# Eight float32 heads instead of ten, and a second set of probability tiles for the others

## The chip, the cores and the metric

The kernel runs on one core of a Trainium2 chip. The metric is the device time of one execution in microseconds (us); the time before is the median of three runs.

## The reference

A block-causal attention (4 batches, 8 heads, 576 positions, 64 wide, blocks of 64) is followed by two dense layers without gates between them: the first squares a ReLU, the second applies a rational function of the hidden value. All data is float32.

```python
def _attn_ref(q, k, v):                      # each (4, 8, 576, 64)
    scores = scale * np.matmul(q, k.transpose(0, 1, 3, 2))
    mask = block_i >= block_j                # blocks of 64
    scores = np.where(mask, scores, -1000000000.0)
    scores = scores - np.max(scores, axis=-1, keepdims=True)
    attn = np.exp(scores)
    attn = attn / (np.sum(attn, axis=-1, keepdims=True) + 1e-09)
    return np.matmul(attn, v)

def _moe_ref(x, w_in, w_out):                # 2304 tokens, 512 -> 2048 -> 512
    h = np.maximum(x @ w_in, 0.0)
    return h * h @ w_out

def _moe2_ref(x, w_in, w_out, a, b):
    h = x @ w_in
    P = a[0] + a[1] * h + a[2] * h * h + a[3] * h ** 3
    Q = 1.0 + np.abs(b[0]) * np.abs(h) + np.abs(b[1]) * h * h
    return (P / (Q + 1e-06)) @ w_out
```

## The kernel before, in words

TensorE multiplies in two ways here. A float32 product keeps its operands as they are. A split product works on a high part in the type fp32r and a remainder (x = high + low), and adds two or three cheaper products. The heads 0 to 9 (PLAIN, L30) are float32 heads ("plain"), the heads 10 to 31 and both dense layers are split.

Attention runs in slots. A slot is one group of query tiles of one head: `GROUPS` (L42) has four, the tiles (0, 1), 2, 3 and 4. The eight heads of batch 0 are visited twice, first for groups 0 and 1 (slots 0 to 15), then for groups 2 and 3 (slots 16 to 31). From then on a head takes four slots: head h has the slots 4h to 4h + 3, up to slot 127. Score tiles are named after their slot: sy68 or sx69 belongs to slots 68 and 69, which are head 17.

The loop at L578 writes down, for slot i: the scores (`emit_s`, TensorE), the division by the row sums of slot i - 1 (`emit_norm`, GpSimd for split heads), the row maximum (`emit_max`, VectorE), the exponential (`emit_exp`, ScalarE, into the probability tiles p0 to p4), the product with the values for slot i - 4 (`emit_pv`), and the transposes of the probabilities of slot i - 3 (`emit_t`, TensorE, copied by ScalarE and, for split heads, a low part taken by VectorE into `pt`). The loads of the following heads and the preparation of their operands (`prep_qk`, `prep_v`) stand in the same loop. A split head costs ScalarE two copies (L234, L235), VectorE one remainder (L238), GpSimd one remainder (L240) and two operations on the values (L249, L251).

The first half of the first dense layer (`moe_a`, hidden units 0 to 1023) is poured in between: `advance` (L544) emits so many steps of three products at each slot, batch by batch. Batch 0 starts at slot 20 (`FIRST`), batches 1, 2 and 3 at the slots 68, 100 and 132. The attention output of a batch, `xt`, is filled head pair by head pair; the hidden products (ha, L482) of a batch read all four pairs in turn, so the last quarter of each waits for the last two heads of the batch. There are two banks of PSUM for these products ("mm", L253).

`convA` (a `Converter`, L81) unpacks the 16 weight tiles of that half, four VectorE operations each (L118 to L122), two ScalarE operations and one on GpSimd. `due` (L562) says at which slots it takes a step: 0.3 steps a slot up to slot 20, then 0.5.

Two sets of probability tiles exist (`psets`, L141), and `ptile` (L158) picks one: heads 0 to 7 take turns, all heads from 8 on use set 0. After slot 36 the pool with the second set, "early", is released (`make_two`, L200), and the tiles q_two and k_two of the split heads take its place.

The program is written in this order, and a scheduler places each engine's instructions from it; each engine then runs its own in the order that results. All loads are issued on SyncE's queue (SP), the first k alone on ScalarE's.

Of the kernel before, what the change touches and what calls it, by code (L numbers as in the profile page):

```python
# [17 lines left out]
P = 128  # L18
# [10 lines left out]
SCALE = 0.125  # L29
PLAIN = 10  # L30
SUBS = ((0, 320), (320, S))
# [5 lines left out]
LN63 = 63.0 * 0.6931471805599453  # L37
MASKED = -1.0e30

# [5 lines left out]
def f(ap):  # L45
    return ap.bitcast(F32)
# [3 lines left out]
def attention_moe_moe(ctx: ExitStack, tc: tile.TileContext, q, k, v, wi1, wo1, wi2, wo2, a, b, out):  # L50
# [107 lines left out]
    def ptile(un, t):  # L158
        own = psets[un.hd % 2 if un.hd < H else 0]
        if un.gis == (0, 1) and un.hd % 4 > 1:  # L160
            return own[4][:, 0:3 * P] if t == 2 else own[3][:, P * t:P * (2 * t + 1)]
        return own[t]
# [9 lines left out]
    class Visit:  # L172
        def __init__(self, n, hd, at, gis):
# [5 lines left out]
            self.k1 = SUB if gis == (0, 1) else S  # L179

    def load_qk(un, eng=nc.sync):
        if len(un.gis) == 2 and un.n % 4 > 1:
# [8 lines left out]
        for q0, q1, k0, k1 in cuts:  # L191
            nc.sync.dma_start(un.qr[:, q0:q1], q[un.hd][:, q0:q1])
            eng.dma_start(un.kr[:, k0:k1], k[un.hd][:, k0:k1])

# [4 lines left out]

    def make_two(un):  # L200
        early.release()
        late = tc.alloc_tile_pool(name="late", bufs=1, reuse_waits="tile")
        for n in range(2):
            q_two.append(late.tile([P, SP], F32R, name=f"q_two{n}"))
            k_two.append(late.tile([P, S], F32R, name=f"k_two{n}"))
            nc.scalar.activation(q_two[n][D:P], un.qr[D:P], AF.Copy)
            nc.scalar.activation(k_two[n][D:P], un.kr[D:P], AF.Copy)
        return late

    def load_v(un):  # L210
        src = v[un.hd].rearrange("p (c d) -> p c d", d=D)
        if un.plain:
            if un.hd % 2 == 0:
                un.vs = attn.tile([P, 5, P], F32, tag="vs", name=f"vs{un.n}", bufs=2)
            else:
                un.vs = units[un.n - 1].vs
            o = D * (un.hd % 2)
            nv = 3 if un.gis == (0, 1) else 5
            nc.sync.dma_start(un.vs[:, 0:nv, o:o + D], src[:, 0:nv])
        else:  # L220
            un.vr = attn.tile([P, 5, D], F32, tag="vr", name=f"vr{un.hd}", bufs=1)
            nc.sync.dma_start(un.vr, src)

    def prep_qk(un, step):
        if un.plain:
            if step == 0 and un.scale == 1.0:
                cols = un.qr[:, un.q0:un.q1]
                nc.gpsimd.tensor_scalar(cols, cols, SCALE, 0.0, op0=ALU.mult, op1=ALU.add)
            return
# [36 lines left out]
    def emit_s(i):  # L266
# [12 lines left out]
        for t in g:  # L279

            cols = slice(P * t, P * (t + 1))
            if un.plain:
                products = [(un.qr[:, cols], un.kr)]
            else:
                products = [(un.qh[:, cols], un.kk), (un.q2[:, cols], un.k2)]
# [126 lines left out]
    def emit_pv(un, half):  # L412
# [13 lines left out]
        if un.plain:  # L426
            for i, (c, src, dst, width) in enumerate(PV[half]):
                for n_, o in enumerate((0, D)):
                    nc.tensor.matmul(ps[o:o + D, dst:dst + width], un.vs[:, c, o:o + D],
                                     un.pt[:, n_, ROW[c], src:src + width],  # L430
                                     start=i == 0, stop=i == len(PV[half]) - 1)
# [127 lines left out]
    AHEAD = 0  # L559
    R1, R2, RS = 0.3, 0.5, 20  # L560

    def due(i):  # L562
        return int(i * R1) if i < RS else int(RS * R1 + (i - RS) * R2)

# [13 lines left out]
    for i in range(NI + 5):  # L578
# [21 lines left out]
        advance(steps(i + 1) - steps(i + 0.5), gate)  # L600
        if i == 4 * PLAIN - 4:
            late = make_two(slots[i][0])
        for back in range(4):
# [16 lines left out]
    if MOE_AT > 4:  # L620
        moes.append(moe_a(B - 1))
    late.release()
    attn.release()
# [261 lines left out]
```

## Time and profile before

| what | us |
|---|---|
| three runs: median (lowest to highest) | 1025.94 (1022.83 to 1026.55) |
| the profiled execution, whole | 1022.03 |
| the profiled execution, span from first to last instruction | 1020.2 |
| slots 0 to 19 and start, no dense layer (0 to 41.2) | 41.2 |
| slots 20 to 39 (41.2 to 93.8) | 52.6 |
| slots 40 to 47, the first two split heads (93.8 to 121.8) | 28.0 |
| slots 48 to 127 (121.8 to 349.3) | 227.5 |
| the rest of attention, `moe_a` of batch 3 (349.3 to 417.8) | 68.5 |
| second half of the first layer, second layer (417.8 to 1020.2) | 602.4 |

A row of the page's first part is an engine's busy time, its share of the span and its instructions. The stretches of the table are cut where a slot's first score product starts on TensorE. TensorE's busy time is modelled at the ends of its products, so a busy TensorE can still be waiting a little; an idle gap before an instruction is shown with what released it.

### The profile page before, as it was taken

The numbers are of one execution on the slowest core, as the hardware profiler recorded it, in microseconds if no ns is written. First come the engines' busy times: TensorE is split into PE (matmuls) and PEld (weight loads), VectorE is DVE, ScalarE is ACT, GpSimd is POOL, SyncE is SP. The second block draws the span as 40 slices with busy tenths as digits, with TensorE's granted clock in tenths as the row PEclk, the third lists the DMA queues.
The fourth block names the chain that finished last, engine by engine and source line by source line (L and its number), as shares of the span: only waits on it lengthen the run. The fifth ranks groups of instructions, "written<-read, shape, count | busy, mean of one in ns | idle before, by whom it ended". The sixth has DMA issues, their size and how long they took to land. (4 is left out here: it accounts for less than half of the span.)

```text
span 1020.2 us, 17058 instructions
## 1 busy us (share of the span) xinstructions
PE 995.7 (98%) x5721; PEld 884.1 (87%) x5721; DVE 727.6 (71%) x1412; ACT 722.2 (71%) x1620; POOL 582.6 (57%) x632
## 2 busy tenths in 40 slices
PE   7999999999999999999999999999999999999997
PEld 5677999999999999999788888887888888899996
DVE  6798587768767646786667666887766766777766
ACT  7779687768777746564455557787787776788775
POOL 5677686768676745630232448767466554655552
PEclk9999999999999999999999999999999999999999
DMA  9766334243432204457655572001101100100000
GB/s 302 221 201 210 120 99 150 92 117 111 118 93 81 67 31 149 167 193 247 234 174 187 171 249 95 1 1 41 42 1 32 42 1 1 50 24 1 32 1 31
DMA packets 63894, 106.58 MB, mean 104 GB/s; under 512 B 16064, under 2 KB 34496, under 8 KB 63808
## 3 DMA queue, kind: packets, MB, share of 16 engines
q1 hardware_dynamic: 63520, 105.34, 32.0%
q8 instruction: 45, 0.74, 0.3%
q14 instruction: 41, 0.34, 0.1%
q10 hardware_dynamic: 288, 0.16, 0.1%
HBM read 79.17 MB, written 23.07 MB: 100 GB/s over the span
## 5 line engine op out<-in xcount | busy, mean ns | idle before, releaser
L816 PE MATMUL yc<-w_co,gc 128*128 128x512 f32 x864 | 211.8, 391 | 3.1 <-ACT gc L776 3.1
L707 PE MATMUL hc<-xc,w_ci 128*128 128x512 f32 (+1 forms) x960 | 211.2, 368 | 0.0
L707 PEld LDWEIGHTS hc<-xc,w_ci 128*128 128x128 f32 x960 | 176.1, 188 | 26.3
L816 PEld LDWEIGHTS yc<-w_co,gc 128*128 128x128 f32 x864 | 161.1, 188 | 36.0 <-ACT gc L776 4.6
L777 POOL TENSOR_TENSOR gc<-t,gc 128x512 fp32r<-128x512 f32 (+1 forms) x78 | 105.0, 1353 | 126.1 <-issue 103.3
L482 PE MATMUL ha<-xt,w_ai 128*128 128x320 f32 (+1 forms) x768 | 123.1, 305 | 0.8 <-POOL xt L451 0.6
L495 PE MATMUL ya<-ga,w_ao 128*128 128x320 f32 (+1 forms) x768 | 117.6, 302 | 3.5 <-ACT r L508 1.9
L482 PEld LDWEIGHTS ha<-xt,w_ai 128*128 128x128 f32 x768 | 107.8, 189 | 5.8 <-issue 3.0
L802 POOL TENSOR_TENSOR wq<-wq,ab 128x512 f32<-128x512 f32 (+1 forms) x78 | 96.4, 1235 | 28.7 <-ACT wq L800 28.7
L495 PEld LDWEIGHTS ya<-ga,w_ao 128*128 128x128 f32 x768 | 107.7, 192 | 5.2 <-ACT r L508 2.1
L747 PE MATMUL yb<-gb,w_bo 128*128 128x512 f32 (+1 forms) x480 | 105.9, 368 | 1.1 <-DVE yp L752 1.1
L707 PE MATMUL hb<-xb,w_bi 128*128 128x512 f32 (+1 forms) x480 | 105.5, 367 | 0.0
L747 PEld LDWEIGHTS yb<-gb,w_bo 128*128 128x128 f32 x480 | 87.6, 188 | 13.1 <-ACT gb L509 1.5
L776 ACT ACTIVATE gc<-t 128x512 fp32r<-128x512 f32 (+1 forms) x80 | 47.1, 589 | 72.9 <-DVE t L785 72.9
L803 DVE TENSOR_TENSOR t<-hc,t 128x512 f32<-128x512 f32 (+1 forms) x80 | 50.9, 636 | 66.0 <-ACT t L801 66.0
L707 PEld LDWEIGHTS hb<-xb,w_bi 128*128 128x128 f32 x480 | 87.4, 188 | 11.2
L356 POOL TENSOR_SCALAR p<-p,stat 64x64 f32<-64x64 f32 (+4 forms) x110 | 62.2, 567 | 43.4 <-DVE stat L352 15.8
L370 PE MATMUL tp<-ident,p 128*128 128x128 f32 x480 | 79.2, 281 | 1.1 <-DVE pt_plain L390 0.7
L783 DVE SCALAR_TENSOR_TENSOR wq<-wq,ab 128x512 f32<-128x512 f32 (+1 forms) x80 | 55.2, 691 | 33.8 <-ACT ab L782 21.9
L402 DVE TENSOR_TENSOR pt<-tp,pt 128x384 fp32r<-128x384 f32 (+3 forms) x176 | 58.8, 366 | 20.3 <-ACT pt L400 17.5
L400 ACT ACTIVATE pt<-tp 128x384 fp32r<-128x384 f32 (+3 forms) x176 | 53.8, 346 | 24.4 <-PE tp L370 22.9
L785 DVE SCALAR_TENSOR_TENSOR t<-t,coef,ab 128x512 f32<-128x512 f32 (+1 forms) x80 | 66.8, 835 | 1.7
(137 smaller groups left out, 1983.2 us busy)
## 6 DMA issues: line engine op xcount, KB each, us to landing
kr<-in_k_dram SPq DMA_DIRECT2D x32, 288.0 KB, 3.8
raw_ci<-in_wi_dram SPq DMA_DIRECT2D x16, 512.0 KB, 4.4
raw_co<-in_wo_dram SPq DMA_DIRECT2D x16, 512.0 KB, 3.6
qr<-in_q_dram SPq DMA_DIRECT2D x24, 320.0 KB, 3.3
raw_ai<-in_wi_dram SPq DMA_DIRECT2D x8, 512.0 KB, 4.8
raw_ao<-in_wo_dram SPq DMA_DIRECT2D x8, 512.0 KB, 4.4
raw_bi<-in_wi_dram SPq DMA_DIRECT2D x8, 512.0 KB, 3.5
raw_bo<-in_wo_dram SPq DMA_DIRECT2D x8, 512.0 KB, 3.4
```

The costliest lines, as they stand in the source:

```text
L356: nc.gpsimd.tensor_scalar(pv, pv, st[r:P, 6 + n:7 + n], 0.0, op0=ALU.mult, op1=ALU.add)
L370: nc.tensor.transpose(ps[:, P * n:P * (n + 1)], ptile(slots[i][0], t)[:, P * c:P * (c + 1)], ident)
L402: nc.vector.tensor_tensor(low, src, f(high), op=ALU.subtract)
L482: nc.tensor.matmul(ps[:, 0:n], w[:, zw, P * kk:P * (kk + 1)], xt[:, zx, kk, first:end], start=i == 0, stop=i == 3 * KK - 1)
L495: nc.tensor.matmul(ps[:, 0:n], wA["o", m][:, zw, P * c:P * (c + 1)], gs[m][:, zg, 0:n], start=i == 0, stop=i == 3 * HALF - 1)
L707: nc.tensor.matmul(ps[:, 0:n], w[:, zw, P * kk:P * (kk + 1)], xt[:, zx, kk, 0:n], start=i == 0, stop=i == 3 * KK - 1)
L747: nc.tensor.matmul(acc[j, c][:, 0:n], wB["o", m][:, zw, P * c:P * (c + 1)], g[:, zg, 0:n], start=m == 0 and i == 0, stop=last and i == 2)
L777: (nc.vector if u - 2 >= len(units) - END else nc.gpsimd).tensor_tensor(g[:, 1, 0:n], t, f(g[:, 0, 0:n]), op=ALU.subtract)
L783: nc.vector.scalar_tensor_tensor(w, w, Q0, r, op0=ALU.add, op1=ALU.mult)
L785: nc.vector.scalar_tensor_tensor(t, t, a0, r, op0=ALU.add, op1=ALU.mult)
L802: (nc.vector if u >= len(units) - END else nc.gpsimd).tensor_tensor(w, w, ab, op=ALU.mult)
L816: last = nc.tensor.matmul(acc[j, c], g[:, zg, P * c:P * (c + 1)], w3["o", m][:, zw, :], start=m == 0 and i == 0, stop=m == NM - 1 and i == 2)
```

## The change

The number of float32 heads goes from ten to eight (heads 8 and 9 become split heads). For the float32 heads the loads and products of q and k use 80 partitions (64 of data and 16 of marks for the mask) instead of 128. The values of a float32 head are loaded as one run of 768 or 1280 bytes a partition instead of runs of 256. `due` becomes one rate, 0.45. The second set of probability tiles stays to the end of attention and all heads take turns. q_two and k_two get places of their own from the start; their mark halves are loaded from DRAM at slot 16 (four loads, four ScalarE copies, two copies by DMA) instead of being copied by ScalarE at slot 36. The mask value becomes a power of two.

```diff
-PLAIN = 10
+PLAIN = 8
-MASKED = -1.0e30
+MASKED = -(2.0 ** 100)
     def ptile(un, t):
-        own = psets[un.hd % 2 if un.hd < H else 0]
+        own = psets[un.hd % 2]
+            self.rows = D + 16 if hd < PLAIN else P
-            nc.sync.dma_start(un.qr[:, q0:q1], q[un.hd][:, q0:q1])
-            eng.dma_start(un.kr[:, k0:k1], k[un.hd][:, k0:k1])
+            nc.sync.dma_start(un.qr[0:un.rows, q0:q1], q[un.hd][0:un.rows, q0:q1])
+            eng.dma_start(un.kr[0:un.rows, k0:k1], k[un.hd][0:un.rows, k0:k1])
-    def make_two(un):
-        early.release()
-        late = tc.alloc_tile_pool(name="late", bufs=1, reuse_waits="tile")
+    def make_two():
         for n in range(2):
-            q_two.append(late.tile([P, SP], F32R, name=f"q_two{n}"))
-            k_two.append(late.tile([P, S], F32R, name=f"k_two{n}"))
-            nc.scalar.activation(q_two[n][D:P], un.qr[D:P], AF.Copy)
-            nc.scalar.activation(k_two[n][D:P], un.kr[D:P], AF.Copy)
-        return late
+            q_two.append(attn.tile([P, SP], F32R, name=f"q_two{n}"))
+            k_two.append(attn.tile([P, S], F32R, name=f"k_two{n}"))
+        for two, src, w_ in ((q_two, q, SP), (k_two, k, S)):
+            for lo in range(0, w_, SUB):
+                hi = min(lo + SUB, w_)
+                raw = attn.tile([P, SUB], F32, tag="tmp", name=f"marks{w_}_{lo}", bufs=2)
+                nc.sync.dma_start(raw[D:P, 0:hi - lo], src[0][D:P, lo:hi])
+                nc.scalar.activation(two[0][D:P, lo:hi], raw[D:P, 0:hi - lo], AF.Copy)
+            nc.sync.dma_start(f(two[1][D:P]), f(two[0][D:P]))
-                un.vs = attn.tile([P, 5, P], F32, tag="vs", name=f"vs{un.n}", bufs=2)
+                un.vs = attn.tile([P, 2, 5 * D], F32, tag="vs", name=f"vs{un.n}", bufs=2)
-            o = D * (un.hd % 2)
-            nv = 3 if un.gis == (0, 1) else 5
-            nc.sync.dma_start(un.vs[:, 0:nv, o:o + D], src[:, 0:nv])
+            nv = D * (3 if un.gis == (0, 1) else 5)
+            nc.sync.dma_start(un.vs[:, un.hd % 2, 0:nv], v[un.hd][:, 0:nv])
-                products = [(un.qr[:, cols], un.kr)]
+                products = [(un.qr[0:un.rows, cols], un.kr[0:un.rows])]
-    R1, R2, RS = 0.3, 0.5, 20
+    RATE = 0.45
     def due(i):
-        return int(i * R1) if i < RS else int(RS * R1 + (i - RS) * R2)
+        return int(i * RATE)
-        if i == 4 * PLAIN - 4:
-            late = make_two(slots[i][0])
+        if i == 4 * H // 2:
+            make_two()
-    late.release()
+    early.release()
     attn.release()
```

The order of the instructions moves with it. TensorE's order where the dense layer passes from batch 0 to batch 1: ha1 are hidden products of batch 1, sx and sy scores (of slots 70 to 73 here), tp the transposes of a slot, pv15 the value product of head 15, the last of batch 0. Before:

```order
L482 MATMUL ha1_0_1_2563<-xt1_1342,w_ai1_349 128x320 x11
L442 MATMUL pv15_1_2476<-pt_1438,vs15_2289 128x192
L370 MATMUL tp64_0_2493<-ident_70,p0_1_91 128x128
L370 MATMUL tp64_0_2493<-ident_70,p1_1_94 128x128
L442 MATMUL pv15_1_2476<-pt_1438,vs15_2289 128x64
L370 MATMUL tp64_0_2493<-ident_70,p1_1_94 128x128
L370 MATMUL tp65_0_2532<-ident_70,p2_1_96 128x128 x3
L482 MATMUL ha1_0_0_2523<-xt1_1342,w_ai0_270 128x320
L482 MATMUL ha1_0_1_2563<-xt1_1342,w_ai1_349 128x320
L294 MATMUL sy70_2611<-kk17_2371,qh17_2370 128x448
```

and of the change, where the end of pv15 and the last products of ha1_0_0 and ha1_0_1 stand:

```order
L296 MATMUL sx73_2839<-kk18_2639,qh18_2638 128x320
L296 MATMUL sx73_2839<-k_two0_545,q_two0_544 128x320
L444 MATMUL pv15_1_2563<-pt_1149,vs15_2376 128x256 x3
L444 MATMUL pv15_1_2563<-pt_1149,vs15_2376 128x192
L372 MATMUL tp64_0_2580<-ident_70,p0_1_91 128x128
L372 MATMUL tp64_0_2580<-ident_70,p1_1_94 128x128 x2
L444 MATMUL pv15_1_2563<-pt_1149,vs15_2376 128x64
L372 MATMUL tp65_0_2619<-ident_70,p2_1_96 128x128 x3
L484 MATMUL ha1_0_0_2610<-xt1_1431,w_ai0_241 128x320 x2
L484 MATMUL ha1_0_1_2650<-xt1_1431,w_ai1_281 128x320 x2
L484 MATMUL ha1_0_0_2610<-xt1_1431,w_ai0_241 128x320
L484 MATMUL ha1_0_1_2650<-xt1_1431,w_ai1_281 128x320
```

Transposes and value products now stand one head (four slots) later against the scores: tp64 follows the scores of slot 73 and not those of slot 69, and with pv15 the last quarter of the first hidden products moves behind slot 73.

ScalarE's order at the first exponential of head 17 (slot 68), p0 being its probability tile and the number behind it the set. Before:

```order
L328 ACTIVATE p4_1_100,stat3_125<-sx67_2460,stat3_125 128x576
L328 ACTIVATE p0_1_91,stat4_126<-sy68_2513,stat4_126 64x64
L445 ACTIVATE tmp15_1_2487<-pv15_1_2476 64x256
L400 ACTIVATE pt_1438<-tp64_0_2493 128x192
L400 ACTIVATE pt_1438<-tp64_0_2493 128x64
L328 ACTIVATE p1_1_94,stat4_126<-sy68_2513,stat4_126 128x192
```

and of the change:

```order
L330 ACTIVATE p4_1_100,stat3_125<-sx67_2547,stat3_125 128x576
L330 ACTIVATE p0_2_106,stat4_126<-sy68_2600,stat4_126 64x64
L402 ACTIVATE pt_1149<-tp60_0_2412 128x192
L447 ACTIVATE tmp14_1_2409<-pv14_1_2398 64x256
L402 ACTIVATE pt_1149<-tp60_0_2412 128x64
L330 ACTIVATE p1_2_109,stat4_126<-sy68_2600,stat4_126 128x192
```

Heads 16 and 17 no longer write the same p0; the copies between the exponentials of slot 68 are those of slot 60 and not of slot 64.

## Rows read from the trace of the kernel before

**Rows 1.** The page: busy us, share of the span, instructions.

```profile
PE 995.7 (98%) x5721; PEld 884.1 (87%) x5721; DVE 727.6 (71%) x1412; ACT 722.2 (71%) x1620; POOL 582.6 (57%) x632
```

**Rows 2.** Stretches: length, busy us by engine, TensorE clock, DMA share, GB/s.

```profile
0.00:41.20 41.20, 34.02 (x174) 23.06 (x175) 26.10 (x76) 28.89 (x97) 23.88 (x61) 0.96 0.82 266
41.20:93.80 52.60, 51.55 (x318) 39.43 (x317) 47.56 (x83) 44.60 (x129) 35.70 (x42) 1.00 0.67 208
93.80:121.80 28.00, 26.32 (x187) 23.23 (x186) 18.56 (x46) 17.62 (x51) 18.78 (x27) 1.00 0.47 144
121.80:226.80 105.00, 101.36 (x790) 99.73 (x790) 78.10 (x245) 79.87 (x243) 73.74 (x107) 1.00 0.39 116
226.80:259.50 32.70, 32.70 (x277) 32.61 (x275) 25.41 (x80) 26.88 (x84) 26.05 (x38) 1.00 0.38 112
349.30:417.80 68.50, 66.50 (x500) 66.09 (x499) 40.72 (x65) 37.69 (x94) 40.32 (x41) 0.98 0.28 92
417.80:1020.20 602.40, 593.81 (x2786) 511.00 (x2784) 426.52 (x620) 417.30 (x717) 297.84 (x227) 1.00 0.24 83
```

**Rows 3.** Groups by shape, whole span: score products and the row-sum transposes.

```profile
L294 PE MATMUL sx<-kk,qh 128*128 128x288 f32 x44 | 13.9, 330 | 0.0
L294 PE MATMUL sx<-k_two,q_two 128*128 128x288 f32 x44 | 12.4, 295 | 0.0
L294 PE MATMUL sx<-kr,qr 128*128 128x288 f32 x40 | 11.6, 412 | 0.1
L436 PE MATMUL rows<-ident,rb 128*128 128x128 f32 x25 | 5.2, 294 | 2.0 <-POOL rb L344 2.0
```

**Rows 4.** Groups on VectorE, whole span: split heads' work, then a weight tile's.

```profile
L402 DVE TENSOR_TENSOR pt<-tp,pt 128x384 fp32r<-128x384 f32 (+3 forms) x176 | 58.8, 366 | 20.3 <-ACT pt L400 17.5
...
L238 DVE SCALAR_TENSOR_TENSOR q_two<-qr,qh 64x640 fp32r<-64x640 f32 x22 | 19.2, 873 | 0.0
...
L122 DVE SCALAR_TENSOR_TENSOR cv_ai<-cv_ai,raw_ai 128x512 uint32<-128x512 uint32 x8 | 6.8, 854 | 0.1
L119 DVE SCALAR_TENSOR_TENSOR raw_ai<-raw_ai 128x512 uint32<-128x512 uint32 x8 | 5.5, 689 | 0.1
L121 DVE TENSOR_SCALAR cv_ai<-cv_ai 128x512 f32<-128x512 f32 x8 | 4.8, 598 | 0.9 <-ACT cv_ai L117 0.9
```

**Rows 5.** DMA issues by line: KB of one, us from issue to landing.

```profile
vr<-in_v_dram SPq DMA_DIRECT2D x22, 160.0 KB, 2.2
k_two<-kk SPq DMA_DIRECT2D x22, 144.0 KB, 2.3
...
qr<-in_q_dram SPq DMA_DIRECT2D x7, 192.0 KB, 4.3
```

**Rows 6.** Groups between 226.8 and 259.5 (three heads): the dense layer's share.

```profile
L482 PE MATMUL ha<-xt,w_ai 128*128 128x256 f32 x96 | 13.6, 285 | 0.0
...
L495 PE MATMUL ya<-ga,w_ao 128*128 128x256 f32 (+1 forms) x50 | 7.2, 286 | 0.0
...
L511 DVE SCALAR_TENSOR_TENSOR s<-ha,r 128x256 f32<-128x256 f32 x8 | 3.4, 419 | 1.4 <-ACT r L508 1.4
```

**Rows 7.** Timeline, 168 to 185: start, us, instruction, idle before it and releaser.

```profile
170.74 0.47 PE L294 MATMUL sy<-kk,qh 128*128 128x448 f32 x1 [1.40 <-ACT p L328]
...
182.02 0.38 PE L370 MATMUL tp<-ident,p 128*128 128x128 f32 x2
...
182.38 0.31 ACT L328 ACTIVATE p<-sy,stat 64x64 f32<-64x64 f32 x1 [3.43 <-issue]
...
184.23 0.47 PE L294 MATMUL sy<-kk,qh 128*128 128x448 f32 x1 [1.02 <-ACT p L328]
```

**Rows 8.** Stretches of 5 us in the start, columns as in rows 2.

```profile
20.00:25.00 5.00, 2.90 (x14) 1.60 (x13) 3.88 (x12) 4.47 (x16) 4.92 (x7) 0.98 0.93 309
25.00:30.00 5.00, 5.00 (x24) 3.14 (x24) 2.14 (x6) 2.92 (x10) 3.71 (x8) 0.68 0.71 244
```

More of the change, by code (lines that the diff above doesn't have):

```diff
@@ L191, in load_qk @@
         for q0, q1, k0, k1 in cuts:
-            nc.sync.dma_start(un.qr[:, q0:q1], q[un.hd][:, q0:q1])
-            eng.dma_start(un.kr[:, k0:k1], k[un.hd][:, k0:k1])
+            nc.sync.dma_start(un.qr[0:un.rows, q0:q1], q[un.hd][0:un.rows, q0:q1])
+            eng.dma_start(un.kr[0:un.rows, k0:k1], k[un.hd][0:un.rows, k0:k1])
     q_two, k_two = [], []
-    def make_two(un):
-        early.release()
-        late = tc.alloc_tile_pool(name="late", bufs=1, reuse_waits="tile")
+    def make_two():
         for n in range(2):
-            q_two.append(late.tile([P, SP], F32R, name=f"q_two{n}"))
-            k_two.append(late.tile([P, S], F32R, name=f"k_two{n}"))
-            nc.scalar.activation(q_two[n][D:P], un.qr[D:P], AF.Copy)
-            nc.scalar.activation(k_two[n][D:P], un.kr[D:P], AF.Copy)
-        return late
+            q_two.append(attn.tile([P, SP], F32R, name=f"q_two{n}"))
[7 more added lines that the diff above has]
+            nc.sync.dma_start(f(two[1][D:P]), f(two[0][D:P]))
     def load_v(un):
-        src = v[un.hd].rearrange("p (c d) -> p c d", d=D)
         if un.plain:
             if un.hd % 2 == 0:
-                un.vs = attn.tile([P, 5, P], F32, tag="vs", name=f"vs{un.n}", bufs=2)
+                un.vs = attn.tile([P, 2, 5 * D], F32, tag="vs", name=f"vs{un.n}", bufs=2)
             else:
                 un.vs = units[un.n - 1].vs
-            o = D * (un.hd % 2)
-            nv = 3 if un.gis == (0, 1) else 5
-            nc.sync.dma_start(un.vs[:, 0:nv, o:o + D], src[:, 0:nv])
+            nv = D * (3 if un.gis == (0, 1) else 5)
+            nc.sync.dma_start(un.vs[:, un.hd % 2, 0:nv], v[un.hd][:, 0:nv])
         else:
             un.vr = attn.tile([P, 5, D], F32, tag="vr", name=f"vr{un.hd}", bufs=1)
-            nc.sync.dma_start(un.vr, src)
+            nc.sync.dma_start(un.vr.rearrange("p c d -> p (c d)"), v[un.hd])
     def prep_qk(un, step):
@@ L226, in prep_qk @@
             if step == 0 and un.scale == 1.0:
-                cols = un.qr[:, un.q0:un.q1]
+                cols = un.qr[0:un.rows, un.q0:un.q1]
                 nc.gpsimd.tensor_scalar(cols, cols, SCALE, 0.0, op0=ALU.mult, op1=ALU.add)
@@ L428, in emit_pv @@
                 for n_, o in enumerate((0, D)):
-                    nc.tensor.matmul(ps[o:o + D, dst:dst + width], un.vs[:, c, o:o + D],
+                    nc.tensor.matmul(ps[o:o + D, dst:dst + width], un.vs[:, n_, D * c:D * (c + 1)],
                                      un.pt[:, n_, ROW[c], src:src + width],
```

## The prediction

> **What bounds the kernel now.** I read the page's engine table first: TensorE is busy 98% of the span, VectorE 71%, ScalarE 71%, GpSimd 57% [rows 1]. Then the stretches between marks of the program [rows 2], because an average over them hides where TensorE really is the limit. From 417.8 on TensorE is busy 593.81 of 602.40 us; the change touches nothing there, so that stretch only starts earlier or later. From 121.8 to 349.3 it is busy almost throughout (32.70 of 32.70 in the three heads from 226.8). Before 121.8 it is another matter: from 41.2 to 93.8 VectorE is busy 47.56 of 52.60 (90%), and in the first 41.2 us TensorE has 34.02 by the model while VectorE has 26.10 and the DMA engines 0.82 of their time. So work taken from TensorE is worth its full price only after 121.8, work added to VectorE costs most between 41.2 and 93.8, and after 121.8 every hole in TensorE's work adds to the end.
>
> The sum is a difference to the profiled execution (1022.0 us). That one lies 3.9 us under the median of the three runs, so I add the difference to the median, 1025.9.
>
> **Part by part.**
>
> *Two heads from float32 to split, on TensorE.* Scores of 288 columns: a float32 head issues four records of 412 ns; a split head four too, two of 330 and two of 295 [rows 3]. That is 1648 - 1250 = 398 ns for 576 columns; a head has 64 + 192 + 320 + 448 + 576 = 1600 columns, so 1.1 us a head, 2.2 for two. The five row-sum transposes of the pair go as well: 5 of 25 in 5.2 us, 1.0 us [rows 3]. The value products keep their number of records, and I count them as equal. Sum: -3.2.
>
> *The same two heads on the other engines.* VectorE gains the low parts of the transposes, 58.8 us over 22 heads = 2.7 a head, the remainder of q, 0.87, and small ones [rows 4]. Least: 3.5 a head. Most: all that VectorE does for a split head. In the three heads from 226.8 that is 25.41 less 3.4 for the dense layer, over three, so 7.3 [rows 2, 6]. Between 7 and 14.6 for two heads; I take 9, nearer the listed rows. Of it one head's low parts (2.7) come after 121.8, since the transposes lag by a head (below).
>
> *Weight tiles at an even pace.* One tile costs VectorE 0.85 + 0.69 + 0.60 and a fourth operation like them, some 2.6 us [rows 4]. By the order eight of the sixteen stand before slot 20 and not five: 7.7 us of VectorE move from the stretch after 41.2 to the one before. After 41.2 this pays for the heads: 9 - 2.7 - 7.7 = -1.4, nothing. Before 41.2 VectorE goes from 26.10 to 33.8 of 41.2 us [rows 2]. Cover is 15 us of idle time there, but it is idle because chains of scores, maximum and exponential wait for each other, and the unpacking stands between them. Bounds 0 and 7.7; I take half, +4. If TensorE's waits there have nothing to do with VectorE, it is 0.
>
> *Loads.* Until slot 20 q and k shrink by 3/8: 8 x (192 + 160) + 2 x (128 + 288) KB become 1368 KB less. Four loads and two copies of marks (608 KB) and one weight tile (512 KB) come in ahead. Net -250 KB, 1 us at the 266 GB/s of that stretch; bounds -5 (1368 KB gone, the rest hidden) and +3. I take 0, as the DMA engines are not full there (0.82) [rows 2]. The third load of marks waits on SP until ScalarE has copied the first (two buffers); behind it on that queue stand a weight tile and the q and k of head 9, so this wait belongs to the same bounds. Longer runs of the values: 0 to -1, in the same bounds.
>
> A row bears on 80 partitions only from afar: a transfer of 64 partitions and 144 KB lands after 2.3 us, one of 128 partitions and 160 KB after 2.2 [rows 5], not slower by much. The Trainium skill speaks against this saving: its page SBUF — State Buffer, "Door 1: The DMA port swizzle", says that 0 to 63 partitions reach only half of the sixteen ports. By that map 80 partitions reach twelve, and the fullest of them still serves as many partitions as with 128. By this rule no time is saved on q and k, the loads would be 1120 KB more, 4 us if all of it showed, and the time 1037; no run here shows 80 partitions yet.
>
> *Two sets of tiles after head 7.* With one set, the exponential of a head's first tile waits for the transposes of the head before. At 182.02 those transposes start, at 182.38 the exponential, after ScalarE idled 3.43 us, and at 184.23 scores on TensorE had waited 1.02 for such an exponential; another 1.40 at 170.74 [rows 7]. Both should go: -2.4. Bounds 0 (the next thing is late as well) and -4.
>
> *What the second set does to the order.* Where nothing holds exponentials back, scores run ahead and transposes and value products fall one head (four slots) behind; in the order the lag grows from slot 38 and is a full head from slot 56. In the steady state this costs nothing. But the hidden products of a batch need the last head pair of that batch. Before, TensorE's order has 408 of the dense layer's products ahead of slot 70 and 480 ahead of slot 76; in the change 402 and 420, and only at slot 80 both have 528. The same comes at batch 2 (840 against 792 ahead of slot 106, equal at 114). So twice one head more passes with almost no dense work to fill TensorE. Such a head costs VectorE 7.3 us (above), 8.1 at the 90% it reaches between 41.2 and 93.8 [rows 2]. On TensorE it is 4.0 us by the rows (32.70 - 13.6 - 7.2, over three) or 5.2 by count (131 of 277 records) [rows 2, 6]; 4.6 between. A hole of 3.5 us, twice: +7.0. Bounds: 0 if the slots ahead had spare work; 2 x 6.9, if such a head keeps the present pace of 10.9 us (32.70 over three).
>
> *The end of attention.* The transposes and value products of two heads instead of one are left behind the last score, and those of the last head have no dense product among them. TensorE needs about 3.7 us for them (31 records at 118 ns); the copies and low parts between are chained. VectorE's part alone is 2.7 [rows 4]. Bounds 0 and 7; I take +2, half of which a trace of the stretch from 349.3 (66.50 of 68.50 busy [rows 2]) leaves open.
>
> *At nothing:* the mask value, a constant; and 80 instead of 128 rows in a float32 product, of which no row shows a case: the sixteen float32 visits keep their number of records and columns, so I take no gain and no loss.
>
> Sum: -3.2 + 4 + 0 - 2.4 + 7.0 + 2 = +7.4, so 1033.3.
>
> **Rivals.** *The holes are filled* (no change): if scores and exponentials that ran ahead give VectorE less to do in those slots, or the hidden products start as early as before, the 7.0 falls away: +0.4, 1026. For it speaks that the lag is a matter of order, and no engine has more work; against it, that TensorE runs its order strictly and the products stand behind pv15 in it.
>
> *Faster:* the start hides the unpacking (0, not +4), loads bring 2, and the end costs nothing: -3.2 - 2.4 - 2 = -7.6 with the holes filled, 1018; with holes of 1 us each, 1020. It decides by the first score of slot 48: if that comes 5 us earlier than 121.8, the holes must eat it. VectorE's 15 us of idle time in the start speak for it.
>
> *The second set changes nothing,* because scores wait for their bank anyway: then the 2.4 stays, 1036.
>
> *TensorE's clock falls in the holes.* From 20 to 25 TensorE is busy 2.90 of 5.00 us, and in the next 5 us the granted clock is 0.68, that is partly at the lower of its two levels, 1.2 GHz [rows 8]. A fall like that costs 0.32 x 5 = 1.6 us; at both holes 3.2: 1036.5. Against it: the holes hold attention's products. The Trainium skill, TensorE: Matmul & The Clock Gate, "What's actually happening", states the same direction (an idle array is throttled, activity releases it); by that rule rows 8 would repeat at the holes, and the trace agrees with it in the start.
>
> **How the numbers follow.** The forecast, 0.40; with a fallen clock or the kept waits, 0.10 together; holes filled, 0.31; faster, 0.19. A difference of 0.5%, 5.1 us, is about what a measurement of this kernel can tell from no change. Slower by more than that (over 1031.0) is the forecast and its two worse forms, 0.50; within it 0.31; faster 0.19. The likeliest case alone spans 1027 to 1044 (start 0 to 7.7, holes 2 x 2 to 2 x 6, end 0 to 5). For 8 in 10 I go down to 1019, where half of the faster case begins, and up to 1044.
>
> **What would show it.** Right: in the trace after, slot 48's first score within 4 us of 121.8; between slots 70 and 76 and between 102 and 108 idle time or stretched records on TensorE with VectorE near 90% busy; no ScalarE gap of 3 us before an exponential of a head's first tile; the second half of the first layer starting some 7 us after 417.8. Wrong: the dense products of batch 1 start as early as before, or the first 121.8 us shrink by more than 5 us, or those stretches show TensorE busy at the pace of before.

## The result, and the profile after

The changed kernel takes 1035.04 us (median of four runs, 1032.19 to 1037.64); the kernel before, on the same chip beside it, 1024.38. The ratio is 1.0119, 95% interval 1.0092 to 1.0147: slower by 1.2%. The profiled execution is the longest of the four, 1037.64, and that of the kernel before, 1022.03, lies under its median; so the stretches below differ by 15.7 us in sum and not by the 10.7 of the medians.

The engine table of the page, to be read against [rows 1], shows more busy time on every engine and nothing that names a cause:

```profile
PE 1002.7 (97%) x5716; PEld 892.4 (86%) x5716; DVE 737.5 (71%) x1440; ACT 728.0 (70%) x1630; POOL 593.3 (57%) x641
```

The stretches do. They are cut at the same marks of the program as [rows 2] (slots 0, 20, 40, 48; slot 20 is cut at its first dense product, 0.4 us behind its first score product), then at the two handovers of the dense layer (slots 64 to 84, 100 to 116), the last score and the second half. Columns: length; busy us on TensorE, its weight loads, VectorE, ScalarE, GpSimd; TensorE clock; DMA share; GB/s.

```profile
0.00:50.50 50.50, 41.73 (x174) 28.88 (x175) 38.77 (x88) 34.33 (x106) 28.22 (x65) 0.93 0.74 220
50.50:101.80 51.30, 49.03 (x319) 38.74 (x318) 47.47 (x92) 43.19 (x126) 37.79 (x46) 1.00 0.67 210
101.80:123.00 21.20, 21.02 (x156) 20.70 (x155) 16.21 (x50) 16.52 (x52) 18.84 (x25) 1.00 0.36 109
163.20:235.50 72.30, 65.45 (x468) 63.64 (x467) 51.01 (x150) 48.42 (x143) 46.11 (x64) 0.95 0.35 105
277.10:333.50 56.40, 52.70 (x382) 51.75 (x382) 37.20 (x110) 38.47 (x115) 35.83 (x52) 0.97 0.30 89
362.30:434.10 71.80, 68.49 (x522) 67.31 (x522) 39.12 (x74) 40.06 (x102) 39.59 (x42) 1.00 0.26 88
434.10:1035.90 601.80, 593.69 (x2786) 511.15 (x2784) 425.21 (x620) 417.68 (x717) 300.57 (x229) 1.00 0.25 83
```

and the two handovers in the kernel before:

```profile
163.40:226.80 63.40, 60.08 (x451) 58.80 (x450) 45.84 (x143) 45.45 (x137) 41.43 (x59) 1.00 0.38 116
270.30:318.90 48.60, 48.60 (x368) 48.45 (x366) 34.10 (x107) 36.88 (x111) 35.31 (x51) 1.00 0.36 105
```

Slot 20 starts at 50.5 instead of 41.2, slot 48 at 123.0 instead of 121.8. The handovers take 72.3 and 56.4 us instead of 63.4 and 48.6. From the last score to the second half it is 71.8 instead of 68.5. The second half then takes what it took before.

The first hole, in the timeline (start, us, instruction, idle time before it and releaser):

```profile
181.49 0.31 ACT L330 ACTIVATE p<-sy,stat 64x64 f32<-64x64 f32 x1 [2.64 <-issue]
183.49 0.47 PE L296 MATMUL sy<-kk,qh 128*128 128x448 f32 x1 [1.46 <-ACT p L330]
187.02 0.30 PE L372 MATMUL tp<-ident,p 128*128 128x128 f32 x1
187.59 1.40 POOL L242 TENSOR_TENSOR kk<-kr,kk 64x576 fp32r<-64x576 f32 x1 [1.56 <-ACT kk L237]
187.63 2.04 DVE L240 SCALAR_TENSOR_TENSOR q_two<-qr,qh 64x640 fp32r<-64x640 f32 x1
190.41 1.25 PE L444 MATMUL pv<-pt,vs 128*128 128x256 f32 x5 [3.10 <-DVE xp L448]
193.46 0.31 ACT L330 ACTIVATE p<-sy,stat 64x64 f32<-64x64 f32 x1 [4.02 <-POOL xt L454]
```

TensorE stands 3.10 us before a value product, which waits for an addition on VectorE (L448), and that addition stands behind the remainder of q (L240), 2.04 us long. The second hole has the same shape: 3.11 us of idle time, up to 289.13. Then the clock falls; five-microsecond stretches around both holes, columns as above:

```profile
185.00:190.00 5.00, 2.17 (x16) 1.68 (x14) 4.49 (x12) 4.34 (x12) 2.42 (x4) 0.98 0.20 53
190.00:195.00 5.00, 4.59 (x21) 4.62 (x22) 2.21 (x8) 1.44 (x6) 3.53 (x6) 0.50 0.54 159
195.00:200.00 5.00, 5.00 (x34) 4.92 (x33) 4.29 (x16) 4.75 (x15) 3.65 (x8) 0.83 0.20 61
285.00:290.00 5.00, 1.77 (x9) 1.56 (x10) 4.71 (x12) 3.10 (x8) 2.47 (x3) 0.88 0.25 52
290.00:295.00 5.00, 4.57 (x28) 4.22 (x27) 2.12 (x7) 2.73 (x11) 3.16 (x5) 0.78 0.47 162
```

### The profile page after: what moved, and what is told of

Read it like the earlier page. It is cut to its first block, busy times and chain, and to the rows that moved or that the text cites. A ratio compares the mean times of both kernels' runs of the same rounds, so it can differ in the third digit from the quotient of the medians.

```text
span 1035.9 us, 17087 instructions
## 1 busy us (share of the span) xinstructions
PE 1002.7 (97%) x5716; PEld 892.4 (86%) x5716; DVE 737.5 (71%) x1440; ACT 728.0 (70%) x1630; POOL 593.3 (57%) x641
## 5 line engine op out<-in xcount | busy, mean ns | idle before, releaser
L358 POOL TENSOR_SCALAR p<-p,stat 64x64 f32<-64x64 f32 (+4 forms) x120 | 68.2, 571 | 43.3 <-DVE stat L354 25.0
L372 PE MATMUL tp<-ident,p 128*128 128x128 f32 x480 | 82.9, 290 | 4.7 <-DVE xp L440 3.7
L404 DVE TENSOR_TENSOR pt<-tp,pt 128x192 fp32r<-128x192 f32 (+1 forms) x192 | 63.5, 366 | 16.3 <-ACT pt L402 10.5
L444 PE MATMUL pv<-pt,vs 128*128 128x256 f32 (+3 forms) x384 | 62.7, 280 | 8.4 <-DVE xp L448 6.7
L402 ACT ACTIVATE pt<-tp 128x192 fp32r<-128x192 f32 (+1 forms) x192 | 57.7, 344 | 18.5 <-PE tp L372 14.6
```

The costliest lines, as they stand in the source:

```text
L358: nc.gpsimd.tensor_scalar(pv, pv, st[r:P, 6 + n:7 + n], 0.0, op0=ALU.mult, op1=ALU.add)
L372: nc.tensor.transpose(ps[:, P * n:P * (n + 1)], ptile(slots[i][0], t)[:, P * c:P * (c + 1)], ident)
L402: nc.scalar.activation(high, src, AF.Copy)
L404: nc.vector.tensor_tensor(low, src, f(high), op=ALU.subtract)
L444: nc.tensor.matmul(ps[:, dst:dst + width], un.vs[:, c, :], un.pt[:, z, ROW[c], src:src + width], start=i == 0, stop=i == len(mm) - 1)
```

## The experiments

Each ratio is to the kernel before on the same chip, with its 95% interval. The other columns come from one profiled execution each: the start of a slot is that of its first score product on TensorE (for slot 20 that of its first dense product, 0.4 to 0.5 us later; in late_dense, which has none there, that of its score product).

| kernel | ratio | slot 20 | slot 48 | 64 to 84 | 100 to 116 | 127 to second half |
|---|---|---|---|---|---|---|
| before | 1 | 41.2 | 121.8 | 63.4 | 48.6 | 68.5 |
| after | 1.0119 [1.0092, 1.0147] | 50.5 | 123.0 | 72.3 | 56.4 | 71.8 |
| one_set | 1.0011 [0.9992, 1.0030] | 51.5 | 126.9 | 63.5 | 48.6 | 68.8 |
| before_two | 1.0126 [1.0090, 1.0161] | 41.6 | 119.8 | 72.0 | 57.1 | 71.4 |
| late_dense | 1.0031 [1.0011, 1.0051] | 49.2 | 118.2 | 59.9 | 47.3 | 81.6 |
| q_first | 1.0103 [1.0068, 1.0137] | 46.9 | 119.6 | 74.6 | 49.4 | 72.1 |
| k_later2 | 1.0143 [1.0104, 1.0182] | 46.0 | 119.1 | 71.0 | 57.1 | 72.0 |
| mix_128 | 1.0011 [0.9997, 1.0025] | 44.8 | 119.9 | 63.4 | 48.6 | 68.4 |
| old_pace | 1.0207 [1.0180, 1.0234] | 48.7 | 128.0 | 71.1 | 57.1 | 72.2 |
| before_even | 1.0003 [0.9989, 1.0017] | 42.7 | 121.8 | 63.4 | 48.6 | 68.2 |
| one_128 | 0.9991 [0.9977, 1.0006] | 42.2 | 120.4 | 63.5 | 48.6 | 67.2 |
| before_80 | 1.0059 [1.0036, 1.0082] | 47.0 | 127.6 | 63.4 | 48.6 | 67.3 |
| products_80 | 0.9996 [0.9976, 1.0016] | 40.1 | 120.8 | 63.4 | 48.6 | 68.5 |
| one_v256 | 1.0006 [0.9988, 1.0024] | 46.7 | 122.9 | 63.4 | 48.5 | 67.4 |

### Is it the second set of tiles? one_set and before_two

One_set takes the second set out of the changed kernel:

```diff
-        own = psets[un.hd % 2]
+        own = psets[un.hd % 2 if un.hd < H else 0]
```

> The changed kernel with one thing undone: from head 8 on all heads use one set of probability tiles again. Theory (lag): the second set lets transposes and value products fall one head behind, and each batch handover of the dense layer then has a head with almost no dense work. With one set TensorE's order has 480 dense products ahead of slot 76 and 840 ahead of slot 106, as before the change (420 and 792 with two sets). Both holes go (8.9 us from slot 64 to 84 and 7.9 us from slot 100 to 116 in the trace of the change), the kept waits return 2 to 3 us: 1019 to 1023 us against 1035 of the change. By the same theory slot 48 then starts later than in the change (123.0), near 126 to 128, since the head owed there has to be paid. Rival (heads): the two extra split heads and the early unpacking cost the time and the order does not matter: 1033 to 1037. Rival (start): the first 50 us lose 9 us that the lag only hides; with one set that shows: 1026 to 1030 with the holes gone.

Before_two puts it into the kernel before, with the places of q_two and k_two from the start and the loads of their marks at slot 16:

```diff
-        own = psets[un.hd % 2 if un.hd < H else 0]
+        own = psets[un.hd % 2]
-        if i == 4 * PLAIN - 4:
-            late = make_two(slots[i][0])
+        if i == 4 * H // 2:
+            make_two()
```

> The kernel before with one thing done: two sets of probability tiles to the end, with the places of q_two and k_two and the loads of their marks as in the change; ten float32 heads, the old pace and loads of 128 partitions stay. TensorE's order has 408 dense products ahead of slot 74 as in the change, not 456. Theory (lag): two holes of about 8 us come, less 2 to 3 us of waits that go: 1035 to 1041 us against 1024 before. Rival (the holes in the change come from the two extra split heads): 1022 to 1027.

Both handovers follow the set and nothing else. One_set, the handovers:

```profile
168.60:232.10 63.50, 60.14 (x452) 58.85 (x451) 46.28 (x143) 45.55 (x137) 41.49 (x59) 1.00 0.38 116
275.50:324.10 48.60, 48.60 (x366) 48.46 (x365) 34.09 (x107) 36.88 (x111) 35.27 (x51) 1.00 0.36 104
```

Before_two, the handovers and the end:

```profile
159.00:231.00 72.00, 65.16 (x468) 63.37 (x467) 50.85 (x148) 47.41 (x142) 45.66 (x64) 0.95 0.34 105
272.60:329.70 57.10, 53.85 (x382) 53.19 (x382) 37.18 (x110) 38.48 (x115) 35.99 (x52) 0.94 0.30 88
358.40:429.80 71.40, 68.52 (x523) 67.38 (x522) 40.66 (x74) 39.64 (x101) 40.45 (x43) 1.00 0.28 90
```

TensorE's busy time, its idle time and the lengths in one_set are those of before within 0.1 us, although it has two more split heads and the even pace. Added alone the set costs 1.26%, taken out it gives 1.08% back: 13 and 11 us, as much as the whole result. In before_two the marks cost nothing either (slot 20 at 41.6). One_set also shows what the lag (transposes and value products falling behind the scores) hid: slot 48 at 126.9, 5.1 us late. That is one execution, at 1026.0 us near the top of the kernel's 1020.1 to 1026.0; its median, 1023.6, lies just above the 1019 to 1023 of the first theory.

### Is it the lag, or the want of dense work? late_dense and q_first

Late_dense keeps the lag of nine slots and starts the dense layer four slots later, so that every head around the handovers has 48 of its products:

```diff
-    MOE_AT = 4
+    MOE_AT = 8
```

> The changed kernel with both sets, but with the first dense layer written four slots later: batch 0 from slot 24, the others at the slots 72, 104 and 136. The lag stays (8 to 9 slots between scores and transposes), but TensorE's order has an even 48 dense products a head through both handovers. Theory (lag): not the lag itself but the want of dense work at the handover costs time; both holes go, and the last heads get dense work between them: 1018 to 1024 us, with slots 64 to 84 and 100 to 116 in the time that they took before the change (51.3 and 48.6 us, plus or minus 2). Rival (the engines cannot keep up at the handover, because VectorE unpacks weight tiles there): 1032 to 1037 with the same stretches 6 us or more longer.

```profile
160.30:220.20 59.90, 57.66 (x447) 56.87 (x445) 45.88 (x139) 45.03 (x135) 43.81 (x61) 1.00 0.42 123
264.90:312.20 47.30, 47.30 (x366) 47.15 (x365) 33.91 (x107) 36.20 (x108) 34.72 (x49) 1.00 0.37 105
343.20:424.80 81.60, 76.55 (x579) 75.43 (x578) 50.12 (x82) 45.81 (x115) 51.07 (x52) 0.98 0.29 92
```

(The 51.3 us in the expectation are slots 64 to 80 of the kernel before, a slip; slots 64 to 84 took 63.4.) The holes are gone with the lag in place, so the rival, that VectorE cannot keep up, falls: the lag costs only where dense work depends on the heads that lag. What is saved comes back in part at the end: 81.6 us instead of 71.8, since 48 dense products are left for it.

Q_first keeps the order of the dense layer and takes away one thing in the hole: GpSimd's remainder of k (L242) waits for VectorE's remainder of q (L240). The cut is shortened at `...`.

```diff
+            seen = attn.tile([P, 1], F32, tag="seen", ...)
+            look = nc.gpsimd.tensor_scalar(seen[0:D], f(un.q2[0:D, 0:1]), 1.0, 0.0, ...)
+            with tc.issue_after(look.ins):
                 nc.gpsimd.tensor_tensor(un.kk[D:P], un.kr[D:P], f(un.kk[D:P]), op=ALU.subtract)
```

> The changed kernel, both sets, with GpSimd's remainder of k made to wait until VectorE's remainder of q is done (GpSimd first copies one column of the result, which adds 24 small operations). In both holes the remainder of q took 2.04 us instead of 0.82 beside GpSimd's remainder of k. Theory (the two block each other): all remainders of q take 0.8 to 0.9 us, TensorE's idle time at the two handovers falls from 3.10 to 1.7 to 2.2 us each, and the time to 1030 to 1034 against 1035. Rival (the remainder of q is long there for another reason): it stays at 2.0 and the time at 1034 to 1037. Other rival (GpSimd's waits cost more than the block did): 1037 to 1042.

The first hole in its timeline:

```profile
185.40 0.81 DVE L240 SCALAR_TENSOR_TENSOR q_two<-qr,qh 64x640 fp32r<-64x640 f32 x1
186.56 1.43 POOL L245 TENSOR_TENSOR kk<-kr,kk 64x576 fp32r<-64x576 f32 x1
186.95 0.73 PE L447 MATMUL pv<-pt,vs 128*128 128x256 f32 x5 [1.85 <-DVE xp L451]
```

The remainder of q falls from 2.04 to 0.81 us and the idle time from 3.10 to 1.85, by the same 1.2 us. The first theory holds for the hole: 1.2 of its 3.1 us was VectorE held up by GpSimd. The Trainium skill, SBUF — State Buffer, "Who interferes with whom", says that a VectorE instruction with two inputs in SBUF and a GpSimd instruction that reads SBUF exclude each other, and that the one issued later waits; the trace agrees: L242 starts at 187.59, L240 at 187.63. The time, 1031.4 us, is in the range of that theory, but the ratios, 1.0103 and 1.0119, do not stand apart by their intervals. The first handover as a whole even takes 74.6 us instead of 72.3: TensorE idles 8.3 us in it instead of 6.9, 1.87 of that in a new hole before a value product at 196.94, and more of the lag is paid back (from slot 64 to 84 the transposes still owed to scored slots fall from 31 to 16, a whole head; in the change from 31 to 24). Nor is the second handover a test of it, as there the lag differs from the start (24 and not 31 transposes owed at slot 100). So what the block costs in time is not shown.

K_later2 tried the same by writing GpSimd's remainder one slot later.

> The changed kernel, both sets, with GpSimd's remainder of k for the next split head written one slot later. At both handovers TensorE idles 3.10 us for an addition on VectorE that stands behind the remainder of q, which took 2.04 us there instead of 0.82, beside GpSimd's remainder of k (1.40 us) that had started a moment earlier. Theory (the two block each other): the remainder of q falls to 0.8 to 0.9 us in both holes, the idle time to 1.8 to 2.2, and with it the fall of the clock behind the hole becomes shorter: 1028 to 1033 us against 1035. Rival (the hole comes from the order alone; another operation fills the time): the holes stay within 0.5 us of 3.1 and the time within 2 us of 1035.

It tells nothing on that point: the scheduler put the operation back beside L240 (2.04 us in both holes, 3.10 idle), and the kernel stayed as slow.

### Does the second set give anything? mix_128

This is one_128 (below) with the second set for the heads 8 to 13 alone; the lag is paid back before the first handover.

```diff
-        own = psets[un.hd % 2 if un.hd < H else 0]
+        own = psets[un.hd % 2 if un.hd < 2 * H - 2 else 0]
```

> one_128 (eight float32 heads, 128 partitions, even pace, one set of tiles from some head on) with the second set kept for the heads 8 to 13, so that the lag grows to 9 slots by slot 56 and is paid back in slots 56 to 64, before the first handover; from slot 64 TensorE's order is that of one_128. Theory (the second set removes waits of 2 to 3 us where there is dense work to fill): 1017 to 1020 us against 1021.1 of one_128, slot 48 at 117 to 119, slot 68 1 to 3 us earlier than 174.4. Rival (scores only run ahead, and paying the lag back takes what it gave): slot 68 within 0.7 us of 174.4 and 1020 to 1023.

Slots 48 to 68, one_128 and then mix_128:

```profile
120.40:174.40 54.00, 51.99 (x427) 51.16 (x426) 42.27 (x135) 43.57 (x133) 37.95 (x56) 1.00 0.40 116
```

```profile
119.90:179.00 59.10, 55.02 (x450) 53.74 (x449) 44.19 (x139) 44.49 (x136) 39.66 (x59) 1.00 0.37 110
```

Slots 40 to 48 take 21.2 instead of 23.0 us, slots 48 to 68 then 59.1 instead of 54.0. Running ahead borrows 1.8 us and pays back 5.1. The theory falls, and the rival was too mild. The time, 0.11% above the kernel before, is not apart from that of one_128 by the intervals.

### Is it the pace? old_pace and before_even

```diff
-    RATE = 0.45
+    R1, R2, RS = 0.3, 0.5, 20
     def due(i):
-        return int(i * RATE)
+        return int(i * R1) if i < RS else int(RS * R1 + (i - RS) * R2)
```

> The changed kernel with the old pace of the weight tiles (0.3 steps a slot up to slot 20, then 0.5). Theory (start): the unpacking moved ahead of slot 20 is what makes slot 20 start at 50.5 and not at 41.2 us; slot 20 then starts at 41 to 45 us. At the end it is worth less, because part of the loss was regained by slot 48 in the change: 1028 to 1033 us against 1035. Rival (loads: 80 partitions and the marks make the start late): slot 20 stays at 48 to 51 and the time at 1034 to 1037.

Before_even is the reverse edit in the kernel before.

> The kernel before with the even pace of the weight tiles alone (0.45 steps a slot). The step of the prediction under test: eight instead of five tiles unpacked ahead of slot 20 cost 4 us (0 to 7.7) there and relieve VectorE behind it by as much. Theory A: a loss of 0 to 4 us at slot 20 that is regained by slot 48, so the time stays at 1020 to 1024 against 1022.4. Theory B (the even pace is what costs the start): slot 20 at 46 to 50 and 1026 to 1031. Theory C (the even pace is a gain of its own, as undoing it in the change cost 8 us): 1016 to 1020.

Theory A of before_even is right: 1.5 us lost at slot 20, none left at slot 48, no change at the end. In the changed kernel the old pace barely mends the start (48.7 against 50.5) and is slower by 0.9%: slots 32 to 48 take 49.7 us (78.3 to 128.0) instead of 42.0. The rival was right on slot 20 and both were wrong on the time, 1043.0 us. With eight float32 heads the first split heads come eight slots earlier, and there the even pace makes room: between slots 32 and 48 VectorE is busy 35.51 us instead of 43.35, GpSimd 38.43 instead of 45.20. GpSimd is the busier of the two, 91% of either stretch; which of them sets the pace was not tried apart.

### Then what makes the start late? one_128, before_80, products_80, one_v256

One_128 is one_set with 128 partitions again (`self.rows = P`).

> The changed kernel with one set of tiles after head 7 (as in one_set) and with loads and products of 128 partitions for the float32 heads again. Compared with one_set, which took 1023.6 us and started slot 12 at 24.7, slot 20 at 51.5 and slot 48 at 126.9. Theory A (80 partitions cost): weight loads on TensorE took twice their usual 190 ns between 9 and 19 us in the traces with 80 partitions and not in those with 128, so the products with 80 rows or their late loads keep the lower clock; slot 12 then starts at 18 to 21 us, slot 20 at 41 to 46, slot 48 at 121 to 124, and the whole takes 1018 to 1021 us. Theory B (80 partitions cost nothing, the eighth weight tile before slot 20 does): slot 12 at 23 to 25, slot 20 at 49 to 52, 1022 to 1026. Theory C (80 partitions save load time): slower than one_set, 1026 to 1030.

Before_80 is the kernel before with 80 partitions (the scaling of q too). Products_80 has of this edit the first line and the last two, 80 rows in the products over whole loads:

```diff
+            self.rows = D + 16 if hd < PLAIN - 1 else P
-            nc.sync.dma_start(un.qr[:, q0:q1], q[un.hd][:, q0:q1])
-            eng.dma_start(un.kr[:, k0:k1], k[un.hd][:, k0:k1])
+            nc.sync.dma_start(un.qr[0:un.rows, q0:q1], q[un.hd][0:un.rows, q0:q1])
+            eng.dma_start(un.kr[0:un.rows, k0:k1], k[un.hd][0:un.rows, k0:k1])
-                products = [(un.qr[:, cols], un.kr)]
+                products = [(un.qr[0:un.rows, cols], un.kr[0:un.rows])]
```

> The kernel before with 80 instead of 128 partitions for the loads and products of q and k of heads 0 to 8 (head 9 keeps 128, since the marks are copied from it); old pace, 256-byte runs of values and one set of tiles after head 7 stay. Theory (80 partitions cost): putting 128 partitions back took one_set from 1023.6 to 1021.1 us, and all traces with 80 partitions show weight loads on TensorE of 333 instead of 190 ns somewhere between 8 and 20 us, which three of four traces with 128 do not; the same doubled loads come here, slot 12 starts at 20 us or later (18.9 before), and the time is 1024 to 1027 against 1022.4. Rival (they cost nothing by themselves, the difference was chance or belongs to the even pace): 1021 to 1023, slot 12 at 18 to 20. Rival (fewer bytes help a start whose DMA engines are busy 0.82): 1017 to 1020.

> The kernel before with score products over 80 rows for heads 0 to 8, while q and k are still loaded and scaled with 128 partitions. It tells apart the two halves of before_80, which took 1028.5 us against 1021.0 and in whose trace the score products' weight loads on TensorE took 334 ns between 8 and 25 us instead of 190 to 200. Theory (the products over 80 rows keep TensorE at the lower of its two clocks): most of those weight loads again take 330 ns, slot 12 starts at 21 us or later (18.9 before, 23.9 in before_80) and the time is 1025 to 1030 us. Rival (the loads with 80 partitions come late and that keeps the array waiting): the weight loads take 190 to 200 ns, slot 12 at 18 to 20, and 1020 to 1023 us.

From 5 to 25 us, before, before_80, products_80; the stretch:

```profile
5.00:25.00 20.00, 16.87 (x87) 11.52 (x87) 16.01 (x44) 16.88 (x63) 11.07 (x17) 1.00 1.00 336
```

```profile
5.00:25.00 20.00, 20.00 (x67) 15.17 (x66) 14.52 (x35) 12.22 (x45) 9.69 (x17) 1.00 0.84 244
```

```profile
5.00:25.00 20.00, 17.93 (x87) 12.96 (x87) 15.83 (x41) 15.30 (x58) 10.65 (x18) 1.00 1.02 326
```

and in the same stretch and order the weight loads of the sy products (busy us, mean ns of one):

```profile
L294 PEld LDWEIGHTS sy<-kr,qr 128*128 128x128 f32 x27 | 4.8, 215 | 0.3 <-POOL qr L228 0.2
```

```profile
L295 PEld LDWEIGHTS sy<-kr,qr 80*128 80x128 f32 x24 | 6.9, 334 | 1.4 <-POOL qr L229 1.0 <-issue 0.2 <-POOL w_ai L111 0.2
```

```profile
L295 PEld LDWEIGHTS sy<-kr,qr 80*128 80x128 f32 x27 | 5.3, 239 | 0.0
```

80 partitions alone make the kernel before slower by 0.59%, 6 us. TensorE runs 67 instead of 87 records in those 20 us and is busy all the time, 0.30 us a record instead of 0.19. With 80 rows in the products but whole loads it issues 87 again, and the time is that of before. So it is not the products by themselves but the loads, alone or together with what goes with them (the products, the scaling of 80 rows), and my theory for products_80 falls.

The rows also show where the time goes. The clock of 1.00 in the stretches of 5 to 25 us is not a reading throughout: the trace's record of the granted clock has its first entry, full speed, at 7.73 us in the kernel before, at 12.88 in products_80 and at 29.37 in before_80, and where it has none the view fills in 1.00 (the 0.96 of [rows 2] and the 0.93 of the change for the stretch up to slot 20 are too high for the same reason; its first entry in the change is at 22.59). Up to that entry the median weight load of the float32 heads' scores takes 333 to 337 ns in all fourteen kernels, in the 6 us behind it 190 to 192. Before_80 behind its first entry:

```profile
L295 PEld LDWEIGHTS sy<-kr,qr 80*128 80x128 f32 x4 | 0.7, 189 | 0.5 <-issue 0.3
```

Where the record does say 0.50, at the holes of the changed kernel, weight loads reach the long form too (shortest, median, longest in ns):

```profile
L296 PEld LDWEIGHTS sy<-kk,qh x72: 186/191/330, 81.0 to 358.7; 128*128 128x128 f32 x72
```

So every kernel starts at the lower of TensorE's two clocks (1.2 and 2.4 GHz), and in before_80 it stays there some 22 us longer than in the kernel before. Over all profiles the time at the lower clock ahead of slot 20 (up to the first entry, and in later falls) is 16.7 to 30.2 us in the eight kernels that load 80 partitions, where slot 20 starts at 46.0 to 51.5 us, and 8.3 to 16.4 us in the six others, where it starts at 40.1 to 44.8. One execution each was traced; among the eight the first entry varies from 12.9 to 29.4 us. Why the clock rises later with these loads stays open: from 5 to 10 us TensorE is busy 4.96 us in the kernel before, where the clock rises, and 5.00 in before_80, where it does not.

In the setting of the change the price is smaller and less sure: one_set to one_128 is 0.2%, with overlapping intervals.

One_v256 is one_set with values in runs of 256 bytes.

> The changed kernel with one set of tiles after head 7 (as in one_set) and with the values of the float32 heads loaded in runs of 256 bytes a partition again. One_set took 1023.6 us. Theory: the longer runs are worth 0 to 1 us, so 1023 to 1026 and slot 20 within 1.5 us of 51.5. Rival: the longer runs are what let the start keep up, so slot 20 moves to 53 us or later and the time to 1027 or more. Other rival: they fill the start's ports at the wrong moment; slot 20 below 49.

0.9988 to 1.0024 against 0.9992 to 1.0030: no difference. Its slot 20, at 46.7, is 4.8 us ahead of one_set's, as the other rival had it, but the time does not follow, and a start in one execution varies: one_128 and mix_128 have the same edits up to slot 32, and slot 20 starts at 42.2 and 44.8 (first clock entry at 8.69 and 12.94).

No kernel beats the one before beyond its interval; one_128 is level with it and 1.3% faster than the change.

## Why the prediction came out, point by point

The forecast was +7.4 us, measured 10.7 between the medians. The mechanism that carried it, two holes at the handovers, is shown by one_set, before_two and late_dense. Several sizes and one cause were wrong, and that the sum came near is in part luck: in the traced pair the holes cost 9.7 us more than forecast, while the stretches between them gave back 4.9 instead of 2.4, and the traced pair differs by 15.7 us, twice the forecast.

*Two holes, 2 x 3.5: too small, 8.9 and 7.8.* They come apart from the rows of the handovers. In the first, the idle time is 72.30 - 65.45 = 6.9 us instead of 3.3 before, so 3.5 more, the figure that I had. A clock of 0.95 over 72.3 us costs 3.6. Two slots of the lag are paid back (31 transposes owed at slot 64, 24 at slot 84, of 15 a head), 1.9 by the 3.7 us a head of the prediction. The sum is 9.0. In the second, 3.7 us are idle, the clock of 0.97 over 56.4 us costs 1.7, and 1.9 are paid back: 7.3 of 7.8. The rival "TensorE's clock falls in the holes" was thus not a rival but a part, at up to 3.6 where it said 1.6. I held attention's products against it; TensorE was busy 2.17 and 1.77 of 5 us there.

That the idle time is 3.5 is luck too. I had it from a VectorE at 90% for a whole head; between slots 70 and 76 it is busy 12.78 of 17.00 us, 75%, and the idle time is one chain, of which 1.2 us is the block that q_first took away:

```profile
183.50:200.50 17.00, 13.76 (x81) 13.12 (x82) 12.78 (x38) 11.84 (x36) 10.54 (x18) 0.80 0.30 84
```

*The second set removes waits, -2.4: wrong.* TensorE still waits 1.46 us for an exponential at 183.49 and ScalarE idles 2.64 and 4.02 before a first tile, against my mark of 3. Stretches between the handovers are shorter by 1.4 (slots 48 to 64), 1.9 (84 to 100) and 1.6 (116 to 127), but the lag grows by some one, two and one slots there, 0.9 to 1.9 us of work put off; mix_128 shows no gain that stays.

*Weight tiles at an even pace, +4 before slot 20: mis-sized.* Before_even lost 1.5 at slot 20 and 0 at slot 48. The other half of that step, that the pace pays for the two heads after 41.2, came out in size: 7.7 us of VectorE by the prediction; with the old pace slot 48 comes 5.0 later although slot 20 comes 1.8 earlier, 6.8 together. The prediction left GpSimd out of it, which was the busier engine there.

*Loads, 0 (-5 to +3): the step that failed.* In the kernel before, 80 partitions alone cost 6 us, outside the bounds; in the changed kernel one_set to one_128 shows 2.5 us, not clear of noise. I had asked only whether fewer bytes save time. They land no sooner; DMA issues of the changed kernel (KB, us to landing):

```profile
qr<-in_q_dram SPq DMA_DIRECT2D x7, 120.0 KB, 4.3
kr<-in_k_dram SPq DMA_DIRECT2D x7, 100.0 KB, 4.5
```

The 192 KB of [rows 5] took 4.3 as well. The Trainium skill, SBUF — State Buffer, "Door 1: The DMA port swizzle", gives the map from partitions to ports, by which 80 partitions reach twelve ports and the fullest serves as many partitions as with 128, so that no time is saved; the rows agree. That TensorE would stay at its lower clock longer beside these loads, neither a row of before nor that map said.

*At nothing, 80 rows in a product:* right, by products_80. *End of attention, +2:* 3.3 (71.8 less 68.5), inside its bounds. *Two heads, -3.2:* not seen by itself. Its 398 ns are worked out from the lengths of records that overlap; from the start of a record to that of the next, the trace of the kernel before has 206 ns on average for the float32 score records of 288 columns, and 168 and 132 for the split ones, so the four differ by 222 ns (an estimate) and the scores of two heads by 1.2 us instead of 2.2. One_128, with the heads, the pace, the marks and the values but neither 80 partitions nor the second set, is 0.09% faster (0.23% faster to 0.06% slower).

So slot 48 came within 4 us of its old place, as the mark asked, for another reason than the one given: in the traces the start loses 5.1 us (one_set), of which the lag put off 3.9.

## What to carry over

A second buffer changes the order before it changes a wait: count in the program's order what falls behind, and look for the place where other work depends on what falls behind. Price a hole on TensorE with the slower clock behind it and the work that is paid back in it, not with its idle time alone. Transfers of fewer partitions need not land sooner: here 80 took as long as 128. A clock of 1.00 in a row is a reading only where the record has an entry; check it by the length of the weight loads.

## What the runs showed of the hardware

- TensorE starts at its lower clock in all fourteen kernels: the median weight load of the float32 heads' scores takes 333 to 337 ns up to the first entry of the clock record (7.7 to 29.4 us), and 190 to 192 right behind it. Ahead of that entry the stretches say 1.00 all the same.
- With loads of 80 partitions that first entry came at 12.9 to 29.4 us (eight kernels), with 128 at 7.7 to 12.9 (six), one execution each.
- A remainder on VectorE that started 0.04 us after one on GpSimd took 2.04 us, and 0.81 when GpSimd waited.
